# A spectral filter and a gated feed-forward block on one core: two sums per channel moved on VectorE, a cosine issued earlier, column transforms moved ahead of the gates

## Chip, cores and metric

The kernel runs on one core of one Trainium2 chip. The metric is device time in microseconds (us), the median of several runs. Engines are named as in the profile: PE is TensorE (matmuls; PEld its weight loads), DVE is VectorE, ACT is ScalarE, POOL is GpSimd, SP is SyncE, which here only issues DMAs.

## What is computed

The input is one matrix of 2048 rows by 576 columns in bf16. The reference, cut to what matters:

```
X = rfft2(layernorm(x)) * (w_r + 1j * w_i)       # over rows and columns
h = x + irfft2(X)
n = layernorm(h)
out = h + (gelu(n @ w_gate) * (n @ w_up)) @ w_down    # 576 -> 4608 -> 576
```

The Fourier transforms are done as matmuls with tables of sines and cosines. The 2048 rows are split as 16 x 128, so that a transform over rows is a 16-point step, a turn by a table, and a 128-point step.

## The kernel before, in words

All engines run hand-ordered queues: the order in the source is the order on each engine, and the tile framework only adds the waits. There are four PSUM tiles of two banks each under the tag "two" (helper `two`, line 66). Every stage below takes its PSUM from this ring. The tiles are handed out in the order in which the program releases them, so allocation number m waits for release number m - 4.

**Start (to about 25 us).** Layer norm of the rows, the 16-point step (`row16`), and the tables. The table TF holds, per channel, minus sine, cosine and sine; it is built in two parts, `first` (two channels) and `rest` (seven). For `rest` the steps are: `angle_a`, `angle_b`, `angle_c` on DVE, `sine` and `cosine` on ACT (lines 252 to 256), `minus_sine` on DVE, and then `turn_tf`, a DMA that writes the turned table TI (line 261).

**Spectral loop (lines 674 to 712, about 25 to 59 us).** The rows' spectrum is handled in eight channels in the order 1, 2, 3, 4, 5, 6, 7, 0; channel k goes together with k + 8. For one channel:

- `f2` (L479) on PE: the transform over columns, six matmuls; `f2_out` (L490) evicts it as `pq`, on ACT except for k = 9, which DVE evicts in two halves.
- `f3` (L496, L497) on PE: two halves of four matmuls with TF. ACT evicts them as `g` and `hs` (L518), except that channel 1's second half stays in PSUM and channel 0's halves are copied straight to `xab`.
- `sums_of` (L527, L528) on DVE: the difference and the sum of `g` and `hs`, which make `xab`.
- `wmul` on DVE: two products with the weights WR and WI (L547, into m1 and m2), `parts` (L552 za, L553 zb), and two writes of the block Zt: the first, L566, and the second, which is not issued there but kept in the list `held` and issued by `release` (L534) behind the two products of the next channel. In channels 6 and 7 it is released at once. Channel 0 is different: it is cut in two column pieces, each with two products and two writes (L575, L578).
- `i3` (L596; L620 for channel 0) on PE: the inverse step from Zt and TI; ACT evicts it into EO (L604, L609). Channels 1 to 4 make EO[0], channels 0 and 5 to 7 make EO[1].

In pass i of the loop PE's order is f2 of channel i, both f3 halves of channel i - 1, f2 of channel i's partner k + 8, then i3 of channel i - 3. DVE's order within `wmul(k, nxt)` before is: product 1, product 2, the previous channel's held write, za, zb, both sums of the next channel, the first Zt write.

**Column transforms.** `inv_cols(x, g)` (L647, ten matmuls on PE) is one inverse transform over columns, x = 0 or 1 for EO[x], g = 0 to 7. ACT evicts it (L660, L669), one of them DVE (L667). Before: (0,0), (0,1), (0,2), then i3 of channel 7, (0,3), (0,4), i3 of channel 0, (0,5), (1,0), (1,1), the 16-point step `add_rows(0)` (L773), (0,6), (0,7), (1,2) to (1,5); the last two, (1,6) and (1,7), stand in the head, described next.

**Feed-forward.** `gate` (L901 to L910): 18 matmuls of one tile of 128 hidden columns, gelu on ACT, product on DVE into P_sb. The rows go in four chunks of 512. Chunk 0 begins with a head of NH = 9 tiles that take only its first 256 rows (lines 912 to 923), so that gates can run before rows 256 to 511 are turned by DMA (`flip`). The main loop then gives these NH tiles their other 256 rows and every later tile all 512. Between the gates of chunk 0, the list `todo`, numbered by the main loop's tile (from 0), issues the remaining rows' work: `fold` (L759, L760, four instructions on DVE), `add_both` (eight matmuls L773 into two PSUM tiles, and two additions L784 on DVE), `stats2` (L116 to L118). Tile 1 has fold(2); tile 4 add_both(2); tile 5 and 6 one stats2 each; tile 6 also fold(3); tile 10 add_both(3) and fold(4). After 36 tiles the down matmuls (L946) follow, then the next chunk.

Of the kernel before, what the change touches and what calls it, by code (L numbers as in the profile page):

```python
# [9 lines left out]
ACT = mybir.ActivationFunctionType  # L10
ALU = mybir.AluOpType
FP32 = mybir.dt.float32
BF16 = mybir.dt.bfloat16
# [7 lines left out]
P = 128  # L21
# [4 lines left out]
J = D // 2 + 1  # L26
JP = J + 1
# [5 lines left out]
JW = 58  # L33
NW = JP // JW
# [3 lines left out]
Y_SCALE = 2.0 / (S * D) / G_SCALE  # L38
# [3 lines left out]
def kernel_body(  # L42
# [12 lines left out]
    V = nc.vector  # L55
    A = nc.scalar
# [9 lines left out]
    def two(name):  # L66
        return psum.tile([P, 2, 512], FP32, name=name, tag="two", bufs=4)
# [83 lines left out]
    WR = sp.tile([P, H + 1, JP], BF16, name="WR")  # L151
    WI = sp.tile([P, H + 1, JP], BF16, name="WI")
# [69 lines left out]
    def drop_sign(dst, src):  # L222
        V.tensor_scalar(
            dst.bitcast(I32),
            src.bitcast(I32),
            1,
            1,
            op0=ALU.logical_shift_left,
            op1=ALU.logical_shift_right,
        )  # L230
# [18 lines left out]
    def angle_c(sl):  # L249
        drop_sign(ab[:, sl], ab[:, sl])  # L250
# [4 lines left out]
    def cosine(sl):  # L255
        A.activation(TF[:, sl, 1, :], ab[:, sl], ACT.Sin, bias=nhpib[:], scale=2.0 * PI / S)
# [98 lines left out]
    first, rest = slice(0, 2), slice(2, 9)  # L355
# [88 lines left out]
    for sign in range(2):  # L444
# [4 lines left out]
            scale=G_SCALE if sign == 0 else -G_SCALE,  # L449
# [5 lines left out]
    wk = spw.__enter__()  # L455
    m1, m2 = (wk.tile([P, 2, 2, JP], BF16, name=n) for n in ("m1", "m2"))
# [5 lines left out]
    xab = {}  # L462
    gk, hk = {}, {}
    zt = {}
    order = [1, 2, 3, 4, 5, 6, 7, 0]
# [6 lines left out]
    def f2(c):  # L472
        ps = two("pq_ps")
        col = slice(slot[c] * P, (slot[c] + 1) * P)
        steps = [(par, t) for par in range(2) for t in (par, par + 2, 4)]
        if c == order[0]:
            steps.sort(key=lambda s: s[1] == 4)
        for par, t in steps:
            T.matmul(  # L479
                ps[:, par, 0:JP],  # L480
                lhsT=Bt[:, t, col],
                rhs=DT[:, t // 2, par] if t < 4 else DF[:, par],
                start=(t == par),
                stop=(t == 4),
            )
        pq[c] = wk.tile([P, 2, JP], BF16, name="pq", tag="pq", bufs=6)
        pq_ps[c] = ps
# [33 lines left out]
            return  # L521
        hk[k] = gh

    def sums_of(k):
        g, hs = gk[k], hk[k]
        x = xab[k] = wk.tile([P, 2, 2, JP], BF16, name="xab", tag="xab", bufs=2)
        V.tensor_tensor(x[:, 0, :, 0:J], g[:, :, 0:J], hs[:, :, 0:J], ALU.subtract)  # L527
        V.tensor_tensor(x[:, 1, ::-1, 0:J], g[:, :, 0:J], hs[:, :, 0:J], ALU.add)  # L528

    held = []  # L530

    def release():
        while held:
            V.tensor_tensor(*held.pop())  # L534

    def wmul(k, i, nxt=None):


        x = xab[k]
        z = Zts[i % 3]  # L540
        zt[k] = z
        zv = z[:].rearrange("p a w b j -> p a b w j")[:, :, :, :, 0:JW]
        sl = slice(k, 18 - k, 17 - 2 * k) if k else slice(0, 9, 8)

        def times(w, m, js):
            n = js.stop - js.start
            V.tensor_tensor(  # L547
                m[:, :, :, js], x[:, :, :, js], w[:, sl, js].unsqueeze(1).to_broadcast([P, 2, 2, n]), ALU.mult
            )

        def parts(za, zb, s):
            V.tensor_tensor(za, m1[:, 0, :, s], m2[:, 1, :, s], ALU.subtract)  # L552
            V.tensor_tensor(zb, m1[:, 1, :, s], m2[:, 0, :, s], ALU.add)  # L553

        def blocks(t):
            return t.rearrange("p b (w j) -> p b w j", j=JW)

        if k:
            times(WR, m1, slice(0, J))
            times(WI, m2, slice(0, J))  # L560
            release()
            za, zb = (wk.tile([P, 2, JP], BF16, name=n, tag=n, bufs=2) for n in ("za", "zb"))
            parts(za[:], zb[:], slice(0, JP))
            if nxt:
                sums_of(nxt)
            V.tensor_tensor(zv[:, :, 0], blocks(za[:]), blocks(zb[:, ::-1]), ALU.add)  # L566
            held.append((zv[:, :, 1], blocks(zb[:]), blocks(za[:, ::-1]), ALU.subtract))
            if k in order[5:7]:
                release()
            return  # L570
        for w0, w1 in ((0, 2), (2, NW)):
            lo, hi = w0 * JW, w1 * JW
            times(WR, m1, slice(lo, min(hi, J)))
            times(WI, m2, slice(lo, min(hi, J)))
            V.tensor_tensor(  # L575
                zv[:, 0, :, w0:w1], blocks(m1[:, 0, :, lo:hi]), blocks(m2[:, 1, :, lo:hi]), ALU.subtract
            )
            V.tensor_tensor(  # L578
                zv[:, 1, :, w0:w1], blocks(m1[:, 1, :, lo:hi]), blocks(m2[:, 0, :, lo:hi]), ALU.add
            )  # L580

    eo = {}

# [55 lines left out]
    cw = {}  # L639

    def inv_cols(x, g):

        ps = two("cs_ps")
        for w in range(NW):
            for e in range(2):
                rows = slice(64 * e, 64 * e + JW)
                T.matmul(  # L647
                    ps[:, e, 0:JP],
                    lhsT=EO[x][rows, w, 2 * g : 2 * g + 2].rearrange("p h e k l -> p (h e k l)"),
                    rhs=DQ[rows, w] if w or e else DT[rows, 0, :, 0, :],  # L650
                    start=(w == 0),
                    stop=(w == NW - 1),
                )
        pv = ps[:, :, 0:JP].rearrange("p t (q a) -> p t q a", q=2)
        if g >= 2:
            if x == 0 or g == 2:
                cw[x, g] = eop.tile([P, 2, JP], FP32, name=f"cw{x}{g}")[:]
            else:
                cw[x, g] = cwb[:, g - 3]
            A.activation(  # L660
                cw[x, g].rearrange("p t (a q) -> p t q a", q=2), pv, ACT.Copy, scale=Y_SCALE
            )
            return
        ts = eop.tile([P, 2, JP], BF16, name=f"cs{x}{g}")
        dst = ts[:].rearrange("p t (a q) -> p t q a", q=2)
        if x == 1 and g == 1:
            V.tensor_scalar(dst, pv, Y_SCALE, None, op0=ALU.mult)  # L667
        else:
            A.activation(dst, pv, ACT.Copy, scale=Y_SCALE)  # L669
        cs[x, g] = ts  # L670
# [4 lines left out]
    for i in range(n + 1):  # L675
        last = i >= n
        if not last:
            f2(order[i])
            if i != 1:
                f2_out(order[i])  # L680
        if i == 0:
            f2(order[0] + 8)
            for r in range(2):
                f2_out(order[0] + 8, V.tensor_copy, slice(r, r + 1))
            angle_c(rest)
            minus_sine(rest)

        if 1 <= i <= n:
            f3(order[i - 1], 0)
            f3(order[i - 1], 1)  # L690
            if i == 1:
                f2_out(order[1])
                sums_of(order[0])
            else:
                if i == 2:
                    cosine(rest)
                    turn_tf(rest)
                    pre = [load_gu(g) for g in range(3)]
                    nc.sync.dma_start(wd_a[:], wd_view[:, 0:NWA, :])
                wmul(order[i - 2], i - 1, order[i - 1])  # L700
        if not last and i:
            f2(order[i] + 8)
            f2_out(order[i] + 8)
        if i >= 3:
            for s in range(3):
                i3(order[i - 3], s)
        if last:
            wmul(order[i - 1], i)
        if i == 1:
            scr_pool.__exit__(None, None, None)  # L710
            eop = ctx.enter_context(tc.tile_pool(name="eop", bufs=1, side="right"))
            EO = [eop.tile([P, 5, H, 2, 4, 8], BF16, name=f"EO{x}", tag=f"EO{x}") for x in range(2)]
    for g in (0, 1, 2):
        inv_cols(0, g)
    for s in range(3):
        i3(order[6], s)
    for g in (3, 4):
        inv_cols(0, g)
    for s in range(3):
        i3(order[7], s)  # L720
    inv_cols(0, 5)

    spw.__exit__(None, None, None)
    spec.__exit__(None, None, None)
# [130 lines left out]
    y0 = add_rows(0)  # L855
    add_sum(0, y0)
    add_sum(1, y0, squares=False)
    for x, g in ((0, 6), (0, 7), (1, 2), (1, 3), (1, 4), (1, 5)):
        inv_cols(x, g)
    A.activation(keep.tile([P, 1], FP32, name="first_gelu")[:], zerob[:], ACT.Gelu_apprx_tanh)  # L860
    junk = roll.tile([P, D], BF16, name="junk", tag="junk", bufs=2)
# [47 lines left out]
        A.activation(g_sb, gu[:, 0, 0:n], ACT.Gelu_apprx_tanh)  # L909
        V.tensor_tensor(p_sb(f)[:, lo:hi], g_sb, gu[:, 1, 0:n], ALU.mult)  # L910

    NH = 9
    after = {
        0: [(sum_squares, 3), (norm2, 2), (flip, 2)],
        1: [(head_rstd, 3)],
# [1 line left out]
    }  # L917
    for f in range(NH):
        gate(0, f, groups[f // FQ], f % FQ, 0, 2 * P)
        for fn, h in after.get(f, ()):  # L920
            fn(h)
        if 2 <= f <= 3:
            inv_cols(1, f + 4)
    for tcnk in range(4):
        for gi in range(NG):
            for i in range(FQ):
                f = gi * FQ + i
                gate(tcnk, f, groups[0], i, 2 * P if tcnk == 0 and f < NH else 0, 4 * P)
                for fn, h in todo.pop(blk, ()):
# [95 lines left out]
```

## Time and profile before

| | us |
|---|---|
| median of 3 runs (lowest, highest) | 498.76 (498.66, 498.78) |
| the profiled execution's own time | 498.63 |
| its span, first to last instruction | 496.9 |
| PE busy in the span | 487.9 (98%) |
| DVE busy | 223.9 (45%) |
| ACT busy | 161.7 (33%) |
| granted TensorE clock, mean | 0.999 |
| gate matmuls L901 on the chain that ended last | 56% |
| down matmuls L946 on that chain | 27% |

Times in the timeline count from the span's start. A row gives the start, the duration, the engine, the line, the operation, the tiles written and read, and, in brackets, how long the engine stood idle before it and what ended that. Durations of two successive rows of one engine overlap: an engine takes up the next instruction a little before the last one's end, so what an instruction costs its engine is the distance between two starts. For example, a sum on DVE lasts 0.46 us, but the next one starts 0.37 us after it.

### The profile page before, as it was taken

How to read it: one execution, taken by the hardware profiler on the slowest of the kernel's cores; microseconds unless marked ns; L12 is line 12 of the kernel's file. 1: busy time of each engine (PE TensorE's matmuls, PEld its weight loads, DVE VectorE, ACT ScalarE, POOL GpSimd, SP SyncE). 2: the span in 40 equal slices, each digit the busy share in tenths (PEclk: the TensorE clock that was granted, in tenths of full speed). 3: DMA queues.
4: the chain of work that ended last, by engine and by line, in shares of the span. 5: the costliest groups of instructions: out<-in, count | busy, mean ns of one | idle time of the engine just before them, and what ended most of it. 6: DMA issues, size and time to landing. Idle time of an engine off the chain costs nothing.

```text
span 496.9 us, 12651 instructions
## 1 busy us (share of the span) xinstructions
PE 487.9 (98%) x5662; PEld 357.5 (72%) x5662; DVE 223.9 (45%) x443; ACT 161.7 (33%) x287; POOL 29.2 (6%) x78
## 2 busy tenths in 40 slices
PE   6999999999999999999999999999999999999997
PEld 3467789888879965555599955555899655555995
DVE  8999786888541245433311254333221333333111
ACT  8989973222311022232300122323110223233000
POOL 8500010211100000000000000000000000000000
PEclk9999999999999999999999999999999999999999
DMA  8729789859990019997730079987700277770000
GB/s 279 226 59 196 206 148 228 158 114 205 214 203 9 2 58 208 190 174 152 151 74 2 3 171 200 181 160 149 145 1 3 77 154 159 155 152 1 15 15 24
DMA packets 89549, 62.33 MB, mean 125 GB/s; under 512 B 23190, under 2 KB 88086, under 8 KB 89494
## 3 DMA queue, kind: packets, MB, share of 16 engines
q1 hardware_dynamic: 89206, 60.34, 60.8%
q0 software_dynamic: 288, 1.18, 0.7%
q8 instruction: 44, 0.72, 0.7%
q14 instruction: 11, 0.09, 0.1%
HBM read 52.65 MB, written 2.36 MB: 111 GB/s over the span
## 4 chain that ended last, share of the span: by engine, by line
PE 92%; ACT 0%; issue 0%; DVE 0%
PE gu L901 56%; PE acc L946 27%; PE cs_ps L647 2%; PE acc L965 2%; PE eo_ps L596 2%; PE pq_ps L479 1%; PE y_ps L773 1%; PE gh_ps L497 0%; PE gh_ps L496 0%; PE eo_ps L620 0%; PE pt L842 0%; ACT g L518 0%; ACT pq L490 0%; ACT hs L518 0%; DVE h_sb L972 0%
## 5 line engine op out<-in xcount | busy, mean ns | idle before, releaser
L901 PE MATMUL gu<-Bt,wgu 64*128 64x512 bf16 (+1 forms) x2646 | 271.9, 363 | 0.0
L901 PEld LDWEIGHTS <-wgu 64*128 64x128 bf16 x2646 | 162.1, 94 | 106.2 <-DMA wgu<-in_B_w_up_dram 0.3
L910 DVE TENSOR_TENSOR P_sb<-g_sb,gu 128x512 bf16<-128x512 f32 (+1 forms) x153 | 99.8, 654 | 143.3 <-ACT g_sb L909 143.3
L909 ACT ACTIVATE g_sb<-gu 128x512 f32<-128x512 f32 (+1 forms) x153 | 87.5, 572 | 193.6 <-PE gu L901 193.3
L946 PEld LDWEIGHTS <-P_sb 64*128 64x128 bf16 x2160 | 132.7, 94 | 0.5
L946 PE MATMUL acc<-wd,P_sb 64*128 64x288 bf16 x1440 | 93.5, 283 | 0.0
L955 DVE TENSOR_TENSOR part<-part,acc 128x576 f32<-128x576 f32 x15 | 11.3, 755 | 111.3 <-ACT part L954 111.3
L946 PE MATMUL acc<-wd_a,P_sb 64*128 64x288 bf16 x720 | 49.4, 283 | 0.0
L954 ACT COPY part<-acc 128x576 f32<-128x576 f32 x15 | 9.6, 639 | 122.4 <-PE acc L946 122.4
L798 DVE TENSOR_SCALAR hrow<-h_sb,mv,rstd 128x1152 bf16<-128x1152 bf16 x14 | 12.2, 868 | 0.6 <-POOL rstd L836 0.6
L479 PE MATMUL pq_ps<-DT,Bt 128*128 128x290 bf16 x64 | 12.3, 287 | 0.0
L901 PE MATMUL gu<-Bt,wgu_e 64*128 64x512 bf16 x108 | 12.2, 376 | 0.0
L286 PE MATMUL f2t<-h_sb,ident 128*128 128x512 bf16 x27 | 8.4, 471 | 3.7 <-DMA h_sb<-in_A_x_dram 3.7
L133 POOL TENSOR_TENSOR rstd<-rstd,mhalf 128x1 f32<-128x1 f32 (+1 forms) x16 | 11.6, 725 | 1.3
L957 DVE TENSOR_TENSOR h_sb<-h_sb,part 128x576 bf16<-128x576 bf16 x15 | 11.4, 758 | 0.5
L901 PEld LDWEIGHTS <-wgu_e 64*128 64x128 bf16 x108 | 10.0, 94 | 1.4
L479 PEld LDWEIGHTS <-Bt 128*128 128x128 bf16 x96 | 9.2, 97 | 2.5
L647 PE MATMUL cs_ps<-DQ,EO 58*128 58x290 bf16 x144 | 11.0, 283 | 0.0
L298 PE MATMUL f2t<-F,xn 128*128 128x256 bf16 x64 | 9.2, 275 | 0.8 <-DVE xn L136 0.8
L490 ACT CAST pq<-pq_ps 128x580 bf16<-128x580 f32 x15 | 9.8, 665 | 0.2
L132 POOL TENSOR_SCALAR rstd<-mv 128x1 f32<-128x1 f32 (+1 forms) x16 | 3.8, 240 | 99.8 <-DVE mv L118 99.5
L647 PEld LDWEIGHTS <-EO 58*128 58x128 bf16 x160 | 8.3, 94 | 1.9 <-issue 0.4
(139 smaller groups left out, 283.6 us busy)
## 6 DMA issues: line engine op xcount, KB each, us to landing
wgu<-in_B_w_gate_dram SPq DMA_DIRECT2D x46, 432.0 KB
wgu<-in_B_w_up_dram SPq DMA_DIRECT2D x46, 432.0 KB
wd_a<-in_B_w_down_dram SPq DMA_DIRECT2D x1, 1728.0 KB
wd<-in_B_w_down_dram SPq DMA_DIRECT2D x1, 1728.0 KB
wd<-in_B_w_down_dram SPq DMA_DIRECT2D x6, 288.0 KB
out_dram<-h_sb SPq DMA_DIRECT2D x3, 576.0 KB
h_sb<-in_A_x_dram SPq DMA_DIRECT2D x4, 288.0 KB
h_sb<-in_A_x_dram SPq DMA_DIRECT2D x2, 576.0 KB
```

Of the source, the lines that this page charges most:

```text
L133: G.tensor_tensor(dst[:, sl], dst[:, sl], mhalf[:, sl], ALU.pow)
L479: T.matmul(ps[:, par, 0:JP], lhsT=Bt[:, t, col], rhs=DT[:, t // 2, par] if t < 4 else DF[:, par], start=(t == par), stop=(t == 4),)
L596: T.matmul(pv[:, n], lhsT=z[:, a, w].rearrange("p b j -> p (b j)"), rhs=TI[:, ts[k], 1 - a : 3 - a, :], start=(a == 0), stop=(a == 1),)
L647: T.matmul(ps[:, e, 0:JP], lhsT=EO[x][rows, w, 2 * g : 2 * g + 2].rearrange("p h e k l -> p (h e k l)"), rhs=DQ[rows, w] if w or e else DT ...
L798: V.tensor_scalar(hrow[:], h_sb[:, h, :].rearrange("p (r k) -> p r k", k=64).unsqueeze(2).to_broadcast([P, NR, 2, 64]), mv2[:, h, 0:1], rs ...
L901: T.matmul(gu[:, c, 0:n], lhsT=w[rows, r, i * P : (i + 1) * P], rhs=hl[tcnk % 2][rows, r, lo:hi], start=(r == 0), stop=(r == NR - 1),)
L909: A.activation(g_sb, gu[:, 0, 0:n], ACT.Gelu_apprx_tanh)
L910: V.tensor_tensor(p_sb(f)[:, lo:hi], g_sb, gu[:, 1, 0:n], ALU.mult)
L946: T.matmul(accs[i][:, c, 0:DH], lhsT=p_sb(f)[rows, st * P : (st + 1) * P], rhs=wd[f // NWA][rows, f % NWA, c * DH : (c + 1) * DH], start=( ...
L955: V.tensor_tensor(part, part, accs[1][:, :, 0:DH], ALU.add)
L957: V.tensor_tensor(hv, hv, part, ALU.add)
L965: T.matmul(acc[:, 0, 0:DH], lhsT=p_sb(f)[:, st * P : (st + 1) * P], rhs=wd[f // NWA][:, f % NWA, cc], start=(f == 0), stop=(f == NFT - 1),)
```

## The change

Five edits, all in the order of the work; no computation is added or dropped.

1. `held` and `release` go. The second Zt write follows the first at once. The two sums of the next channel, before side by side between zb and the first Zt write, are dealt out: the difference behind the two products, the sum behind zb.
2. Channel 0 is no longer cut: two products over all columns, two writes.
3. `cosine(rest)` is issued in pass 0, behind `f2_out` of channel 1 on ACT, instead of in pass 2. `angle_c(rest)` moves ahead of DVE's two copies for k = 9, since the cosine reads its result.
4. (0,5) and (0,6) go ahead of i3 of channel 0, so that seven transforms stand before it; (0,7) follows it; (1,2) to (1,7) follow `add_rows(0)`. None is left in the head. DVE evicts (0,6) instead of ACT.
5. NH becomes 11.

```diff
     def wmul(k, i, nxt=None):
...
+        times(WR, m1, slice(0, J))
+        times(WI, m2, slice(0, J))
         if k:
-            times(WR, m1, slice(0, J))
-            times(WI, m2, slice(0, J))
-            release()
+            if nxt:
+                sum_of(nxt, 0)
             za, zb = (wk.tile([P, 2, JP], BF16, name=n, tag=n, bufs=2) for n in ("za", "zb"))
-            parts(za[:], zb[:], slice(0, JP))
+            parts(za[:], zb[:])
             if nxt:
-                sums_of(nxt)
+                sum_of(nxt, 1)
             V.tensor_tensor(zv[:, :, 0], blocks(za[:]), blocks(zb[:, ::-1]), ALU.add)
-            held.append((zv[:, :, 1], blocks(zb[:]), blocks(za[:, ::-1]), ALU.subtract))
-            if k in order[5:7]:
-                release()
-            return
-        for w0, w1 in ((0, 2), (2, NW)):
...
+            V.tensor_tensor(zv[:, :, 1], blocks(zb[:]), blocks(za[:, ::-1]), ALU.subtract)
+        else:
+            V.tensor_tensor(zv[:, 0], blocks(m1[:, 0]), blocks(m2[:, 1]), ALU.subtract)
+            V.tensor_tensor(zv[:, 1], blocks(m1[:, 1]), blocks(m2[:, 0]), ALU.add)
...
         if i == 0:
             f2(order[0] + 8)
+            angle_c(rest)
+            cosine(rest)
             for r in range(2):
                 f2_out(order[0] + 8, V.tensor_copy, slice(r, r + 1))
-            angle_c(rest)
             minus_sine(rest)
...
-                    cosine(rest)
                     turn_tf(rest)
...
-    for g in (3, 4):
+    for g in (3, 4, 5, 6):
         inv_cols(0, g)
     for s in range(3):
         i3(order[7], s)
-    inv_cols(0, 5)
+    inv_cols(0, 7)
...
-    for x, g in ((0, 6), (0, 7), (1, 2), (1, 3), (1, 4), (1, 5)):
+    for x, g in [(1, g) for g in range(2, 8)]:
         inv_cols(x, g)
...
-    NH = 9
+    NH = 11
...
-        if 2 <= f <= 3:
-            inv_cols(1, f + 4)
```

`sum_of(k, half)` is `sums_of` split in two: half 0 allocates `xab` and writes the difference, half 1 writes the sum.

More of the change, by code (lines that the diff above doesn't have):

```diff
@@ L522, in f3, with sum_of @@
         hk[k] = gh
-    def sums_of(k):
+    def sum_of(k, half):
         g, hs = gk[k], hk[k]
[L526 to L534, printed above, removed]
+        if half == 0:
+            xab[k] = wk.tile([P, 2, 2, JP], BF16, name="xab", tag="xab", bufs=2)
+        x = xab[k]
+        V.tensor_tensor(
+            x[:, 1, ::-1, 0:J] if half else x[:, 0, :, 0:J],
+            g[:, :, 0:J],
+            hs[:, :, 0:J],
+            ALU.add if half else ALU.subtract,
+        )
     def wmul(k, i, nxt=None):
@@ L549, in times, with parts @@
             )
-        def parts(za, zb, s):
-            V.tensor_tensor(za, m1[:, 0, :, s], m2[:, 1, :, s], ALU.subtract)
-            V.tensor_tensor(zb, m1[:, 1, :, s], m2[:, 0, :, s], ALU.add)
+        def parts(za, zb):
+            V.tensor_tensor(za, m1[:, 0], m2[:, 1], ALU.subtract)
+            V.tensor_tensor(zb, m1[:, 1], m2[:, 0], ALU.add)
         def blocks(t):
             return t.rearrange("p b (w j) -> p b w j", j=JW)
+        times(WR, m1, slice(0, J))
+        times(WI, m2, slice(0, J))
         if k:
-            times(WR, m1, slice(0, J))
-            times(WI, m2, slice(0, J))
-            release()
+            if nxt:
+                sum_of(nxt, 0)
             za, zb = (wk.tile([P, 2, JP], BF16, name=n, tag=n, bufs=2) for n in ("za", "zb"))
-            parts(za[:], zb[:], slice(0, JP))
+            parts(za[:], zb[:])
             if nxt:
-                sums_of(nxt)
+                sum_of(nxt, 1)
             V.tensor_tensor(zv[:, :, 0], blocks(za[:]), blocks(zb[:, ::-1]), ALU.add)
-            held.append((zv[:, :, 1], blocks(zb[:]), blocks(za[:, ::-1]), ALU.subtract))
-            if k in order[5:7]:
-                release()
-            return
-        for w0, w1 in ((0, 2), (2, NW)):
[L572 to L580, printed above, removed]
+            V.tensor_tensor(zv[:, :, 1], blocks(zb[:]), blocks(za[:, ::-1]), ALU.subtract)
+        else:
+            V.tensor_tensor(zv[:, 0], blocks(m1[:, 0]), blocks(m2[:, 1]), ALU.subtract)
+            V.tensor_tensor(zv[:, 1], blocks(m1[:, 1]), blocks(m2[:, 0]), ALU.add)
     eo = {}
@@ L659, in inv_cols @@
                 cw[x, g] = cwb[:, g - 3]
-            A.activation(
-                cw[x, g].rearrange("p t (a q) -> p t q a", q=2), pv, ACT.Copy, scale=Y_SCALE
-            )
+            dst = cw[x, g].rearrange("p t (a q) -> p t q a", q=2)
+            if x == 0 and g == 6:
+                V.tensor_scalar(dst, pv, Y_SCALE, None, op0=ALU.mult)
+            else:
+                A.activation(dst, pv, ACT.Copy, scale=Y_SCALE)
             return
@@ L692, in kernel_body @@
                 f2_out(order[1])
-                sums_of(order[0])
+                sum_of(order[0], 0)
+                sum_of(order[0], 1)
             else:
                 if i == 2:
-                    cosine(rest)
                     turn_tf(rest)
```

## The prediction, made blind

> **What bounds the kernel now.** I read the page's first part, then the windows by stage, then the timelines of DVE, ACT and PE around each edit.
>
> ```profile
> PE 487.9 (98%) x5662; PEld 357.5 (72%) x5662; DVE 223.9 (45%) x443; ACT 161.7 (33%) x287; POOL 29.2 (6%) x78
> ```
>
> Over the whole span PE is the bound, and behind the spectral loop its queue runs on almost without idle time. So an edit counts only through PE's idle time. The loop itself reads differently. Columns of the windows: length, then busy us of PE, PEld, DVE, ACT, POOL, then clock, DMA share, GB/s.
>
> ```profile
> 32.00:36.00 4.00, 3.00 (x23) 1.85 (x21) 4.00 (x10) 3.66 (x6) 0.00 (x0) 1.00 0.28 57
> 40.00:44.00 4.00, 4.00 (x37) 3.25 (x34) 4.00 (x10) 3.88 (x8) 0.00 (x0) 1.00 1.12 214
> 48.00:52.00 4.00, 4.00 (x35) 3.08 (x33) 4.00 (x11) 3.91 (x8) 0.00 (x0) 1.00 1.13 203
> ```
>
> From 40 to 52 us PE **and** DVE are full. By starts, one channel costs DVE two products of 0.67 and six adds of 0.37, 3.57 us; PE 20 matmuls (f2, f3) of 0.124 and ten (i3) of 0.109, also 3.57. At 32 to 36 PE idles 1 us, and DVE doesn't. PE's idle time, by its timeline:
>
> ```profile
> 32.80 0.30 PE L496 MATMUL gh_ps<-pq,TF 128*128 128x289 bf16 x1 [0.27 <-ACT TF L256]
> 33.33 0.28 PE L497 MATMUL gh_ps<-pq,TF 128*128 128x289 bf16 x1 [0.23 <-ACT pq L490]
> 35.61 0.60 PE L596 MATMUL eo_ps<-TI,Zt 128*128 128x256 bf16 x4 [0.51 <-ACT hs L518]
> ```
>
> By distance of starts less 0.12, these lost 0.43 (the cosine), 0.41 (a `pq` that stood behind the cosine on ACT) and 0.67. The third row names ACT's `hs`, but that was done at 35.13; what ended just before 35.61 is DVE's held write:
>
> ```profile
> 34.38 0.76 DVE L547 TENSOR_TENSOR m<-xab,WI 128x1156 bf16<-128x1156 bf16 x1
> 35.05 0.46 DVE L534 TENSOR_TENSOR Zt<-zb,za 128x580 bf16<-128x580 bf16 x1
> ```
>
> It ends at 35.51. So edits 1 and 3 aim at 1.5 us of PE's idle time. The end of the loop decides whether that is kept. DVE, then PEld:
>
> ```profile
> 51.59 0.45 DVE L534 TENSOR_TENSOR Zt<-zb,za 128x580 bf16<-128x580 bf16 x1
> 52.10 0.99 PEld L596 LDWEIGHTS <-Zt 128*128 128x128 bf16 x10 [0.25 <-DVE Zt L534]
> ```
>
> Channel 6's i3 starts 0.06 behind the write that DVE ends at 52.04, and DVE has run without a gap since 28.78. **PE leaves the loop when DVE does.**
>
> **Edit 3, the cosine.** ACT:
>
> ```profile
> 26.72 0.64 ACT L490 CAST pq<-pq_ps 128x580 bf16<-128x580 f32 x1
> 28.10 0.64 ACT L518 CAST g<-gh_ps 128x578 bf16<-128x578 f32 x1 [0.74 <-PE gh_ps L497]
> 31.68 1.07 ACT L256 ACTIVATE TF<-ab,nhpib 128x896 bf16<-128x896 f32 x1
> ```
>
> `angle_c` (0.62) fits DVE's 0.56 of idle time ahead of 26.83: its input ends at 26.27, it runs from 26.30, its start-to-start 0.53 ends at 26.83. The cosine then starts at 26.72 + 0.54 = 27.26, and `g` 0.945 later (as 31.68 to 32.63), at 28.20 instead of 28.10. That `g` opens DVE's chain: first difference at 28.88 instead of 28.78. Cost: 0.10 at DVE's head. Gain on PE: channel 3's f3 no longer waits (32.38 instead of 32.80; a rest of 0.03 for `pq` stays). SP's order is unchanged: `turn_tf` stands behind thirteen small DMAs that SP issues until 33.98.
>
> **Edit 1, the sums.** Channel 1's products then start at 30.40 and 31.08. The next difference is wanted at 31.75, but its `hs` (ACT, 31.15 for 0.66) ends at 31.81: start 31.85, a new wait of 0.09. It replaces a gap of 0.19 before (product 2 from 30.98 to za at 31.84 instead of 0.67 later, since za reads product 2 directly). Then za 32.22, zb 32.59, sum 32.96, writes 33.33 and 33.70, next product 34.07. Before, the products started at 33.70 with a write of 0.37 still owed, which is 34.07 too. From there the instruction count is the same, 3.57 us per channel: channel 7's first product comes at 34.07 + 5 x 3.57 = 51.93, against 51.96. **DVE gains 0.03.**
>
> Behind the waiting difference on DVE are za and zb. In later channels `hs` is early enough: PE runs ahead, channel 3's `hs` ends near 34.3 for a difference at 35.42, and from channel 4 on the margin is 0.7 us.
>
> PE: i3 of channel 1 now waits for a write that ends at 34.16: start 34.24, 1.37 earlier. It keeps this lead at 3.57 us per channel until its two f3 halves of channel 0 end at 50.62. Then i3 of channel 6 wants the write that ends at 51.56 + 0.46 = 52.02: start 52.07. **The lead of 1.37 turns into a wait of 1.45 there**; net gain 0.03.
>
> By occupancy this reads otherwise. The Trainium skill, Perfetto Trace Analysis, section "Identifying the Most-Contended Engine", tells to improve the engine with the highest occupancy and to look for gaps on it; by the page that is PE, and its gaps of 1.5 us would be the gain: 497.1 without the other edits. The windows above do not bear that out for this stage, where DVE has none to give; the same page's "Optimization Strategy" allows for regimes with different engines.
>
> **Edits 2 and 4.** Uncut, channel 0 costs DVE 0.67 + 0.79 + 0.37 + 0.46 from 55.08: done at 57.4, against 57.95. PE asks for it later than before (57.83): i3 of channel 7 at 55.25, four transforms of 0.62, so 59.0. Nothing waits for DVE there, before or after; the 0.21 between the matmuls at each of the four changes between i3 and transforms (53.09 to 53.30 is one) is the same whoever is named, so I read 0.08 of it as a switch that stays. With two transforms in place of four, PE would be at 57.8 and still not wait. The two transforms leave the head, where each took 0.63 (71.03 to 71.66): gain 0.02. Evictions keep up: the one given to DVE (about 0.82, as L667) ends at 60.0, for a PSUM tile wanted at 60.3. The loads of `wgu_e` wait for i3 of channel 0 and issue 1.2 later, near 60.5; their traffic, which ended near 70.5 in the windows, ends near 72. The head's tiles 9 and 10 now read them, from 78.
>
> **Edit 5, NH.** A half tile takes PE 0.983 (180 matmuls in 9.83), a whole one 1.943 (108 in 11.65): two tiles cut cost 2 x (1.966 - 1.943) = 0.05. But the cut also speeds PE through tiles 9 and 10 while DVE is behind:
>
> ```profile
> 88.73 0.45 DVE L759 TENSOR_TENSOR both<-cwb 128x288 bf16<-128x288 f32 x1
> 89.10 0.45 DVE L760 TENSOR_TENSOR both<-cwb 128x288 bf16<-128x288 f32 x1
> 89.47 0.75 DVE L910 TENSOR_TENSOR P_sb<-g_sb,gu 128x256 bf16<-128x256 f32 x2
> 90.39 0.69 DVE L910 TENSOR_TENSOR P_sb<-g_sb,gu 128x512 bf16<-128x512 f32 x1 [0.17 <-ACT g_sb L909]
> ```
>
> DVE is full from 83.81 to 90.2 with add_both(2), two stats2 and fold(3); only then come the products of tiles 7 and 8 (ends 89.88 and 90.21). PE:
>
> ```profile
> 83.58 4.19 PE L901 MATMUL gu<-Bt,wgu 64*128 64x256 bf16 x72
> 87.51 4.15 PE L901 MATMUL gu<-Bt,wgu_e 64*128 64x512 bf16 x36
> 91.40 0.75 PE L773 MATMUL y_ps<-both,G 64*128 64x288 bf16 x8
> ```
>
> Tiles 9 and 10 take 3.89 whole, 1.97 as halves. So, counted from the main loop's start, add_both(3) comes at 91.40 - 1.92 = 89.48, with its second matmul at 89.58. By the ring its two PSUM tiles are those of tiles 7 and 8. Tile 8's is free at 90.21, plus 0.06 to 0.10 as at the waits above: **a new wait of 0.70 us**. Afterwards DVE is ahead and PE waits no more: tile 11's PSUM (tile 9's, 90.54) is free when PE gets there at 90.7.
>
> The bounds of this term: 0, if the tiles handed out are others; 1.4, if tile 10's own product had to pass too (two half products of 0.33 behind 89.80, so 90.46 + 0.41 = 90.87; less 89.58, plus 0.1). I take 0.70, since the rows of tiles 7 and 8 give it.
>
> **Sum**, on the profiled execution (498.63, of which 496.9 span and 1.7 around it): - 0.03 (DVE's chain) - 0.02 (head) + 0.05 (halves) + 0.70 (wait) = + 0.70: 499.33. The median of the runs shown is 0.13 above that execution: **499.4 to 499.5; I say 499.4**, + 0.14%. A difference of about 0.2%, 1.0 us, is what I take as measurable.
>
> **Rivals.**
> - *The wait at tile 10 doesn't come* (a PSUM tile is free earlier): 498.76 + 0.0 = 498.8. Against it stand the two DVE rows; for it, that no row of before shows that wait.
> - *The lead is kept* (the rule above as a mechanism: the loop is PE's, DVE shortens with the dealt order): - 1.4 for the three waits. With the wait at tile 10, 498.0; without, 497.4. Against it: DVE's gapless chain.
> - *Slower: the early difference waits in every channel.* It stands 1.34 us into the channel's DVE time, before 2.45; `hs` came only 0.03 to 0.13 ahead of it in rows 39.76 to 50.48. If PE does not get its lead of 1.37 (say the cosine lands later, or `hs` stays where it was), DVE loses 1.11 less 0.1 once, then runs in step. It decides when channel 3's `hs` ends later than 35.4; I expect 34.3. Price + 1.0, all on PE behind channel 6: 500.4.
> - *The change does not do what it says*: the waits at 32.80, 33.33 and 35.61 remain; without lead or loss the time is that of my forecast within 0.1, since DVE sets the end.
>
> **Chances.** Forecast (499.0 to 499.8) 0.62; no wait at tile 10: 0.13; lead kept: 0.05 with and 0.05 without that wait; difference late: 0.12; the rest, 0.03, slower for a cause not seen. The range takes in the forecast, the case without the wait and the late difference, 0.87: 498.6 to 500.5. Faster by over 0.2% (under 497.8) is the lead kept without the wait, 0.05, and a little of that with it, 0.02: 0.07. Slower (over 499.8): 0.12 + 0.03 and the forecast's upper edge 0.03: 0.18. Within: 0.75.
>
> **What would show it.** Right: `g` of channel 1 near 28.2; i3 of channel 1 near 34.2; PE idle for about 1.4 ahead of i3 of channel 6, which starts within 0.1 of 52.1; no idle time at i3 of channel 0; PE idle 0.6 to 0.8 within add_both(3), released by DVE's P_sb. Wrong: DVE idle ahead of differences from channel 3 on; i3 of channel 6 ahead of 51.5; add_both(3) without a wait.

## The result, and the profile after

The changed kernel takes **499.53 us** (median of 22 runs, 499.15 to 500.5); 22 runs of the kernel before beside them gave 498.67 (498.44 to 499.34). The ratio is 1.0018, with a 95% interval of 1.0012 to 1.0025: slower by 0.86 us, where + 0.7 was forecast. The profiled execution took 499.36, 0.17 below the median; its span is 497.6 (before 496.9).

The whole start lies about 0.1 us earlier in this execution (the first f3 matmul starts at 27.32, before at 27.41), so times forecast on the old time axis are read here less 0.1. The windows of the loop in the kernel after, columns as before (length, busy us of PE, PEld, DVE, ACT, POOL, clock, DMA share, GB/s):

```profile
32.00:36.00 4.00, 4.00 (x35) 3.04 (x34) 4.00 (x10) 3.50 (x6) 0.00 (x0) 1.00 0.63 59
...
48.00:52.00 4.00, 2.74 (x25) 2.01 (x23) 4.00 (x10) 3.82 (x7) 0.00 (x0) 1.00 1.13 200
```

PE's idle microsecond at 32 to 36 is gone, and 1.26 us of idle time have come up at 48 to 52, where PE was full. DVE is full in both windows, before and after.

**Where PE gained.** PE's timeline at the first i3:

```profile
32.28 0.28 PE L496 MATMUL gh_ps<-pq,TF 128*128 128x289 bf16 x1
32.43 0.28 PE L497 MATMUL gh_ps<-pq,TF 128*128 128x289 bf16 x1
...
33.91 0.28 PE L479 MATMUL pq_ps<-DF,Bt 128*128 128x290 bf16 x1
34.16 1.25 PE L587 MATMUL eo_ps<-TI,Zt 128*128 128x256 bf16 x10
```

The first two starts are 0.15 apart (0.12 is normal: the 0.03 foretold), and i3 of channel 1 starts at 34.16 instead of 35.61, 0.13 late against its predecessor. The waits of 0.43, 0.41 and 0.67 are gone. DVE at the same place:

```profile
28.77 1.43 DVE L529 TENSOR_TENSOR xab<-g,gh_ps 128x578 bf16<-128x578 bf16 x2 [0.85 <-ACT g L518]
...
30.97 0.76 DVE L547 TENSOR_TENSOR m<-xab,WI 128x1156 bf16<-128x1156 bf16 x1
31.75 0.47 DVE L529 TENSOR_TENSOR xab<-g,hs 128x578 bf16<-128x578 bf16 x1
...
33.61 0.45 DVE L568 TENSOR_TENSOR Zt<-zb,za 128x580 bf16<-128x580 bf16 x1
```

The early difference starts 0.78 behind the second product instead of 0.67: it waits for `hs` by 0.11, once. The second write now stands behind the first and ends at 34.06; i3 starts 0.10 behind it.

**Where PE lost it.** First DVE, then PE, at the end of the loop:

```profile
51.46 0.46 DVE L568 TENSOR_TENSOR Zt<-zb,za 128x580 bf16<-128x580 bf16 x1
```

```profile
50.43 0.29 PE L497 MATMUL gh_ps<-pq,TF 128*128 128x289 bf16 x1
51.98 1.27 PE L587 MATMUL eo_ps<-TI,Zt 128*128 128x256 bf16 x10 [1.26 <-DVE Zt L568]
```

From 50.43 to 51.98 are 1.55 us, of which a matmul costs 0.12: PE waits 1.43 for the write that ends at 51.92. Counted from the first f3, i3 of channel 6 starts at 24.66, before at 24.69. All of PE's lead is gone but 0.03.

**Where the time went.** DVE, then PE, around add_both(3) in the feed-forward:

```profile
90.93 0.45 DVE L754 TENSOR_TENSOR both<-cwb 128x288 bf16<-128x288 f32 x1
91.30 1.41 DVE L904 TENSOR_TENSOR P_sb<-g_sb,gu 128x256 bf16<-128x256 f32 x4
```

```profile
89.35 2.23 PE L895 MATMUL gu<-Bt,wgu_e 64*128 64x256 bf16 x36
91.77 0.98 PE L767 MATMUL y_ps<-both,G 64*128 64x288 bf16 x8 [0.19 <-DVE P_sb L904]
```

The four products on DVE are those of tiles 7 to 10; they stand in DVE's queue behind all of fold(3). Tile 7's ends at 91.72 and lets add_both(3) start at 91.77; tile 8's ends at 92.05 and lets its second matmul start at 92.10. These two matmuls start 0.463 and 0.330 behind their predecessors. In add_both(2) of the same kernel, which waits for nothing, the same two steps are 0.006 and 0.103. So 0.46 and 0.23 are lost, **0.68 us** in all. The bracket names only 0.19, since modelled matmul ends hide the rest; the distance of starts shows it.

A second, small loss was not foretold. The list of waits of the kernel after has

```profile
PEld L895 <- DMA wgu<-in_B_w_up_dram: 0.4, 1, 0.4
```

The gate matmul at 137.00 starts 0.315 behind the one at 136.69, and its tile of 18 matmuls takes 0.11 longer than the 1.94 of the others: lost to a weight load (before, this wait of PEld was 0.3 and cost PE nothing).

From anchor to anchor (us):

| from, to | before | after | difference |
|---|---|---|---|
| first f3 to i3 of channel 6 | 24.69 | 24.66 | - 0.03 |
| to the first gate | 15.99 | 17.23 | + 1.24 (two more transforms) |
| to the first down matmul | 74.32 | 73.91 | - 0.41 |

The two transforms take 1.25 out of the third stretch; 0.68 for the wait, 0.11 for the load and 0.05 for the cut tiles come in, which makes the - 0.41. The sum of the three stretches is + 0.80.

### The profile page after: what moved, and what is told of

Its sections match the earlier page's. It is cut to its first block, busy times and chain, and to the rows that moved or that the text cites. A ratio compares the mean times of both kernels' runs of the same rounds, so it can differ in the third digit from the quotient of the medians.

```text
span 497.6 us, 12727 instructions
## 1 busy us (share of the span) xinstructions
PE 487.6 (98%) x5698; PEld 340.2 (68%) x5698; DVE 224.5 (45%) x442; ACT 161.6 (32%) x288; POOL 28.9 (6%) x78
## 4 chain that ended last, share of the span: by engine, by line
PE 88%; DVE 7%; DMA 2%; SPq 1%; ACT 1%; issue 0%
PE gu L895 55%; PE acc L938 27%; PE cs_ps L638 2%; PE acc L957 2%; DVE m L547 2%; DMA h_sb<-in_A_x_dram 1%; PE y_ps L767 1%; SPq L421 1%; DVE xab L529 1%; DVE xn L136 1%; DVE st L117 1%; DVE st L116 1%; DVE Zt L567 0%; PE eo_ps L587 0%; ACT Bt L322 0%
## 5 line engine op out<-in xcount | busy, mean ns | idle before, releaser
L895 PEld LDWEIGHTS <-wgu 64*128 64x128 bf16 x2646 | 144.8, 94 | 123.6 <-DMA wgu<-in_B_w_up_dram 0.4
L895 PE MATMUL gu<-Bt,wgu_e 64*128 64x256 bf16 (+1 forms) x144 | 12.5, 322 | 0.0
L587 PE MATMUL eo_ps<-TI,Zt 128*128 128x256 bf16 x70 | 8.8, 273 | 1.3 <-DVE Zt L568 1.3
L123 ACT ACTIVATE junk<-h_sb 128x576 bf16<-128x576 bf16 x14 | 9.4, 678 | 0.4 <-DMA h_sb<-in_A_x_dram 0.4
```

The lines of the kernel that those rows point to most:

```text
L895: T.matmul(gu[:, c, 0:n], lhsT=w[rows, r, i * P : (i + 1) * P], rhs=hl[tcnk % 2][rows, r, lo:hi], start=(r == 0), stop=(r == NR - 1),)
```

## The experiments

**Theory.** (W) What makes the change slower is the wait in add_both(3), which comes from NH = 11 together with the folds ahead of it in DVE's queue. (D) Edits 1 and 3 give PE a real lead of 1.4 us, and it is worth nothing as DVE ends the loop and PE has nothing else to do there. **Rivals**: the loss lies in the cut tiles or the moved loads and not in that wait; PE's idle 1.43 us is harmless and what PE does there doesn't matter; the lead isn't the edits' doing.

Runs of the kernel before stand beside every experiment's (medians 498.54 to 498.62); ratios are to these.

**1. NH = 11 alone, on the kernel before**

```diff
-    NH = 9
+    NH = 11
```

> The kernel before with NH = 11 alone, no other edit. Theory W: the waits of 0.4 and 0.2 us appear in add_both(3) here too, so 0.6 to 0.7 us over before: 499.3 to 499.4. Rival L: no change, 498.7.

Measured: 499.35 (499.19 to 499.6), ratio 1.0014 [1.0005, 1.0023]. PE's timeline:

```profile
91.80 0.98 PE L773 MATMUL y_ps<-both,G 64*128 64x288 bf16 x8 [0.19 <-DVE P_sb L910]
```

Steps of 0.463 and 0.332 at the two first matmuls, as in the changed kernel (0.463 and 0.330). From the first f3 to the first down matmul: 115.71, before 115.00, after 115.80. One constant gives nearly all of the loss, with none of the other four edits.

**2. The folds ahead of the wait, on the changed kernel.** fold(2) and fold(3) go from the main loop's tiles 1 and 6 into the head, behind its tiles 6 and 8.

```diff
-            todo.setdefault((1, 6, 10, 13, 16, 19)[h // 2 - 2], []).append((fold, h // 2))
+            if h > 6:
+                todo.setdefault((10, 13, 16, 19)[h // 2 - 4], []).append((fold, h // 2))
...
+        6: [(fold, 2)],
+        8: [(fold, 3)],
```

> The changed kernel with fold(2) and fold(3) issued in the head, behind tiles 6 and 8, where DVE idles 0.56 us per tile, in place of tiles 1 and 6 of the main loop. Theory W: DVE is no longer behind at tile 7, the waits in add_both(3) go, nothing else moves: 0.6 us off the changed kernel, 498.9. Rival L: no change, 499.5.

Measured: 498.71 (498.46 to 499.61), ratio 1.0004 [0.9995, 1.0013]. PE's timeline (this execution began 0.87 us later than that of the changed kernel):

```profile
90.22 2.23 PE L896 MATMUL gu<-Bt,wgu_e 64*128 64x256 bf16 x36
92.19 0.75 PE L767 MATMUL y_ps<-both,G 64*128 64x288 bf16 x8
```

add_both(3) starts 1.97 us behind the first of the 36 half matmuls of tiles 9 and 10, and two half tiles take 2 x 0.983; in the changed kernel it was 2.42. No bracket is left. First f3 to first down matmul: 115.17, 0.63 less than after: the wait's 0.68 is gone, and the late weight load costs 0.16 here instead of 0.11. The medians differ by 0.82, the lowest runs by 0.69. The wait goes with its cause, so (W) holds against the cut tiles, which are still there.

**3. Fewer tiles cut: NH = 10, and NH = 9**

```diff
-    NH = 11
+    NH = 10
```

> The changed kernel with NH = 10 in place of 11, nothing else. Theory W (the loss is PE's wait in add_both(3), since tiles 9 and 10 as halves bring PE there before DVE has released the PSUM of tiles 7 and 8): tile 10 is whole again, PE arrives 0.96 us later, the waits of 0.40 and 0.23 in add_both(3) are gone; but the second halves now begin at about 79.0 us, where the turned rows land at about 79.2, so up to 0.4 of it may come back there: 498.9 to 499.3. Rival L (the loss is in the spectral loop, the wait of 1.4 us ahead of channel 6's i3): no change, 499.5.

Measured: 499.27 (498.85 to 499.84), ratio 1.0011 [1.0002, 1.0020]. The wait in add_both(3) is gone, but PE's timeline has another:

```profile
79.94 5.09 PE L895 MATMUL gu<-Bt,wgu 64*128 64x256 bf16 x90 [0.53 <-DMA Bt<-hrow]
```

The matmul at 79.94 starts 0.80 behind the one at 79.14, and its tile loses 0.80 us: the head ends before the rows turned by DMA are there. The last DMA packets of the turn end at 79.2, but in the trace its last semaphore update comes at 79.81, and PE goes on 0.13 behind that. The expectation went by the packets and allowed 0.4. From the first f3 to the first down matmul this kernel takes 115.78, the changed one 115.80: what one wait gives back the other takes.

```diff
-    NH = 11
+    NH = 9
```

> The changed kernel with NH = 9. Theory W: no wait in add_both(3), but with no transforms left in the head the second halves begin at 78.05 us, ahead of the turned rows (79.2): a new wait of 1.1 to 1.3 us on a DMA in its place, 500.0 to 500.2. Rival L: no change, 499.5. A third view, that NH is of no matter: 499.5 too.

Measured: 500.08 (499.81 to 500.42), ratio 1.0028 [1.0017, 1.0039]. The step from the matmul at 78.31 to the next, at 80.00, loses 1.69, where 1.1 to 1.3 were expected:

```profile
80.00 4.21 PE L895 MATMUL gu<-Bt,wgu 64*128 64x256 bf16 x74 [1.42 <-DMA Bt<-hrow]
```

Here too PE goes on 0.13 behind the turn's last semaphore update (79.87). In the changed kernel that update comes at 79.78, in the kernel before at 77.93.

So edit 5 isn't a slip. With two transforms taken out of the head, it needs two more tiles until the rows are there; with 11 tiles the main loop starts at 80.01 without a wait, 0.10 behind the time at which it could. The cover has a price of 0.68 further on, and without it edit 4 costs 0.80 (10) or 1.69 (9) at once.

**4. The wait at the loop's end filled.** The transforms (0,0) and (0,1) go ahead of i3 of channel 6; three then stand ahead of channel 7's, two ahead of channel 0's. Alone on the changed kernel:

```diff
+        if last:
+            for g in (0, 1):
+                inv_cols(0, g)
...
-    for g in (0, 1, 2):
+    for g in (2, 3, 4):
...
-    for g in (3, 4, 5, 6):
+    for g in (5, 6):
```

> The changed kernel with the filled wait alone, the folds where the change has them. Theories D and W together: 1.25 us off the changed kernel's 499.5 and the waits of 0.6 in add_both(3) stay: 498.2 to 498.3, so that the two repairs add up. If PE's wait in add_both(3) grew or vanished because PE comes earlier: 497.5 or over 498.8.

Measured: 498.10 (497.91 to 498.96), ratio 0.9988 [0.9979, 0.9997]; add_both(3)'s steps of 0.46 and 0.33 stay. Together with the folds of experiment 2:

> The changed kernel with the folds in the head (as before) and PE's order at the loop's end changed: transforms (0,0) and (0,1), whose input has been ready since channel 4, go ahead of channel 6's i3, into PE's wait; (0,2) to (0,4) then stand before channel 7's i3, (0,5) and (0,6) before channel 0's. Theory D: PE's lead of 1.4 us is real, it was only lost for want of other work; 1.24 us of transforms fill the wait, channel 0's i3 starts near 57.7 instead of 58.95, and the time is 497.4 to 497.5, faster than both kernels. Rival P: the order doesn't matter, 498.7 as with the folds alone.

Measured: **497.44** (497.22 to 498.27), ratio 0.9976 [0.9966, 0.9986]: faster than both kernels. PE's timeline at the loop's end:

```profile
50.64 0.29 PE L497 MATMUL gh_ps<-pq,TF 128*128 128x289 bf16 x1
50.87 0.79 PE L638 MATMUL cs_ps<-DQ,EO 58*128 58x290 bf16 x9
51.50 0.78 PE L638 MATMUL cs_ps<-DQ,EO 58*128 58x290 bf16 x9
52.22 1.26 PE L587 MATMUL eo_ps<-TI,Zt 128*128 128x256 bf16 x10
```

The whole start lies 0.2 later in this execution (first f3 27.53). The transforms run where PE had waited, and i3 of channel 6 is not held up by them: it starts 24.69 behind the first f3. By medians the folds give 0.8, the fill 1.4, both 2.1. So (D) holds: PE's idle time there was real, and other work put into it uses it.

The same fill on the kernel before:

```diff
+        if last:
+            for g in (0, 1):
+                inv_cols(0, g)
...
-    for g in (0, 1, 2):
+    for g in (2,):
```

> The kernel before with the same two transforms ahead of channel 6's i3, no other edit. Theory D: PE had no lead there (its wait was 0.11 us), so at most 0.1 us comes off: 498.5 to 498.6. A third view, that the order of the transforms is worth something by itself: as much as in the changed kernel, 1.2 us off, 497.4.

Measured: 498.65 (498.52 to 499.05), ratio 1.0002 [0.9993, 1.0011]. i3 of channel 6 moves to 53.44, 1.34 later, about what the two transforms take: with no lead there is nothing to fill.

**5. Which edit makes the lead.** Each kernel is that of folds and fill with one edit undone.

Edit 1 undone:

```diff
         times(WI, m2, slice(0, J))
         if k:
-            if nxt:
-                sum_of(nxt, 0)
+            release()
...
+                sum_of(nxt, 0)
                 sum_of(nxt, 1)
...
-            V.tensor_tensor(zv[:, :, 1], blocks(zb[:]), blocks(za[:, ::-1]), ALU.subtract)
+            held.append((zv[:, :, 1], blocks(zb[:]), blocks(za[:, ::-1]), ALU.subtract))
+            if k in order[5:7]:
+                release()
```

> The same kernel (497.44), with edit 1 undone: sums side by side, the second write held behind the next channel's products. Theory D: channel 1's i3 waits for the held write at 35.6 again and PE has no lead left, whatever the cosine does, so the filling transforms only push channel 6's i3 back: all of the 1.25 us is lost, 498.7. Rival: the early cosine alone made the lead, 497.4 to 498.0.

Measured: 498.81 (498.66 to 499.5), ratio 1.0005 [0.9996, 1.0014]. i3 of channel 1 is back at 35.58, and i3 of channel 6 comes late:

```profile
53.41 1.27 PE L595 MATMUL eo_ps<-TI,Zt 128*128 128x256 bf16 x10
```

Edit 3 undone:

```diff
-            angle_c(rest)
-            cosine(rest)
             for r in range(2):
                 f2_out(order[0] + 8, V.tensor_copy, slice(r, r + 1))
+            angle_c(rest)
...
+                    cosine(rest)
                     turn_tf(rest)
```

> The kernel with folds in the head and filled wait (497.44), with edit 3 undone: angle_c and the cosine are back in their places of before. Theory D: PE loses 0.43 and 0.41 us at channel 3's f3 again, its lead at channel 1's i3 is 0.7 instead of 1.4 us, so the filling transforms end near 52.6 instead of 51.9 and channel 6's i3 is late by 0.6: 498.0. Rival: the dealt order alone made the lead, 497.4.

Measured: 498.09 (497.96 to 498.33), ratio 0.9986 [0.9977, 0.9995]. PE's waits of 0.43 (for the cosine) and 0.41 (for the `pq` behind it) are back, i3 of channel 1 starts at 34.84, that of channel 6 at 52.62.

Edit 2 undone (channel 0 in two pieces again):

```diff
+            for w0, w1 in ((0, 2), (2, NW)):
...
+                times(WR, m1, slice(lo, min(hi, J)))
+                times(WI, m2, slice(lo, min(hi, J)))
```

> The same kernel (497.44), with edit 2 undone: channel 0 cut in two column pieces again. DVE ends it near 58.0 instead of 57.4, and PE asks for its first piece at 57.7, for the second at 58.2. Theory D: no wait, 497.4 within 0.1. Rival (the uncut channel was needed): a wait of 0.3 to 0.6 at channel 0's i3, 497.7 to 498.0.

Measured: 497.47 (497.28 to 497.72), ratio 0.9975 [0.9964, 0.9985]; i3 of channel 0 at 57.94 waits for nothing.

So without edit 1 the fill gives nothing (498.81); edit 3 is worth 0.65 of the lead beside it; edit 2 nothing.

**6. Is DVE the bound of the loop?** Four of its sums are left out of DVE's queue, so that part of the spectrum is missing, and memsets on POOL stand in.

```diff
+        if half and k in (3, 4, 5, 6):
+            G.memset(x[:, 1, :, 0:J], 0.0)
+            return
```

> The changed kernel without the sums of channels 3 to 6: each is left out, and POOL writes zeros in its place, so that part of the spectrum is lost; DVE has four adds of 0.37 us less inside the loop. Theory D (DVE sets the end of the loop, and edits 1 and 3 only moved PE's idle time to the wait ahead of channel 6's i3): that wait of 1.4 us goes, channel 6's i3 starts near 50.6, and 1.4 us come off: 498.1 by the median of the changed kernel (499.5). Rival P (PE or ACT sets the loop's pace, DVE's adds are covered): no change, 499.5.

Measured: 498.54 (498.39 to 499.43), ratio 1.0000 [0.9991, 1.0009]: faster than the changed kernel by 1.0, less than expected. Counted from the first f3, i3 of channel 6 comes 0.72 earlier and not 1.48 (4 x 0.37). DVE's timeline shows why:

```profile
36.29 0.45 DVE L556 TENSOR_TENSOR zb<-m,m 128x580 bf16<-128x580 bf16 x1
36.78 0.46 DVE L570 TENSOR_TENSOR Zt<-za,zb 128x580 bf16<-128x580 bf16 x1
```

With the sum between them gone, the write that reads zb starts 0.49 behind it, not 0.37 (up to 0.56 in other channels): the sum had covered 0.12 to 0.19 of waiting for a result, 0.61 in the four channels. Channel 7's difference waited 0.12 for its `hs` besides. Together these are 0.73 of the 0.76 that are missing. The direction is that of DVE as the bound: what came off DVE's chain came off PE's wait, whose bracket is 0.59 instead of 1.26. The size of the expectation was wrong. From the first f3 to the first down matmul the gain is 0.84, since the late weight load costs nothing here.

**7. Work of DVE handed to POOL**

```diff
-        V.tensor_tensor(
+        (G if k in (3, 4, 5, 6) and not half else V).tensor_tensor(
```

> The changed kernel with the differences of channels 3 to 6 on POOL, which is idle in the loop; nothing is left out. Theory D: if POOL works beside DVE, four adds of 0.37 us come off DVE's chain and up to 1.4 us off the whole: 498.1. If the two engines hinder each other while both read SBUF (the Trainium skill, SBUF - State Buffer, section Who interferes with whom, says that a DVE instruction with two SBUF inputs contends with a POOL instruction that reads SBUF), DVE's adds and products grow longer by about what POOL takes, and nothing is gained or some is lost: 499.5 to 501. Rival P: 499.5.

Measured: 502.6 (502.46 to 502.74), ratio 1.0078 [1.0065, 1.0092]. POOL, then DVE:

```profile
38.50 1.87 POOL L529 TENSOR_TENSOR xab<-g,hs 128x578 bf16<-128x578 bf16 x1 [1.74 <-ACT hs L518]
```

```profile
38.48 0.75 DVE L547 TENSOR_TENSOR m<-xab,WR 128x1156 bf16<-128x1156 bf16 x1
39.16 1.84 DVE L547 TENSOR_TENSOR m<-xab,WI 128x1156 bf16<-128x1156 bf16 x1
```

The product that starts 0.02 ahead of POOL's instruction keeps its 0.75; the one that starts while POOL computes takes 1.84 instead of 0.76 and ends at 41.00, 0.63 behind POOL's end at 40.37, about as if it had begun then. A za beside another of POOL's took 1.42 instead of 0.46. It goes the other way too: POOL's first of the four, at 34.52, took 2.24, where its shortest took 1.28, while two products of DVE kept their 0.76. i3 of channel 6 comes at 55.43. The Trainium skill, SBUF — State Buffer, section "Who interferes with whom", has the rule: a DVE instruction with two inputs from SBUF contends with a POOL instruction that reads SBUF, and not with one that only writes it. Both runs agree: beside the memsets of experiment 6 (0.58 us each on POOL) the adds kept 0.45 to 0.46.

## Why the prediction was right

- **DVE ends the loop: right, as the main step.** i3 of channel 6 was to keep 0.03 of 1.37; it kept 0.03 of the 1.35 by which i3 of channel 1 came earlier against the first f3. The wait was forecast at 1.45 and is 1.43. (The chain "without a gap" of before holds by the profile's brackets; by starts DVE waited 0.18 and 0.19 for its own results at 30.30 and 31.84, and the second of these is the gap that the prediction itself counts under edit 1.) Experiments 4 and 5 show that the lead existed and what it was worth.
- **Edit 3**: `g` of channel 1 was to come at 28.20 and the first difference at 28.88, so 28.10 and 28.78 on the new axis. ACT, kernel after:

```profile
27.14 1.06 ACT L256 ACTIVATE TF<-ab,nhpib 128x896 bf16<-128x896 f32 x1
28.09 0.65 ACT L518 CAST g<-gh_ps 128x578 bf16<-128x578 f32 x1
```

  So 28.09, and 28.77 for the difference (above). The cosine went into the 0.74 us for which ACT had waited ahead of `g`, and cost only what stood over.
- **Edit 1**: difference of channel 2 late by 0.11 (forecast 0.09), channel 7's first product at 51.83 (51.93 less 0.1), no wait at a difference in channels 3 to 6. The rival of the difference late in every channel did not come.
- **Edits 2 and 4**: i3 of channel 0 at 58.95 without a wait (59.0 forecast), DVE's eviction of (0,6) from 59.05 to 59.8 (to 60.0 forecast).
- **Edit 5**: the step was the wait of two PSUM tiles' releases in add_both(3), and its size is near the forecast: 0.68 for 0.70. The tiles are those of 7 and 8, as derived from the ring. Experiments 1 and 2 put it in and took it out.
- **What the sum lacked**: the weight load that costs 0.11 at 137.00. The prediction followed the moved `wgu_e` loads only up to the head. Whether it is these loads that make the later one late isn't shown: kernels that issue the same loads lose nothing there (experiment 4, both) or 0.16 (experiment 2).
- **Luck at the turned rows**: the prediction has no term for the rows that DMA turns. In the changed kernel they come 1.85 later than before (79.78 against 77.93), and the head ends 0.10 behind the time at which PE could take them. So the term is nothing, but by a margin that the prediction never looked at; experiment 3 shows what a shorter head would have cost.
- **From + 0.70 to + 0.86**: the three stretches give + 0.80, which is the forecast with 0.11 for the load and 0.02 less for the wait. The two profiled executions differ by only 0.73, mainly because that of the changed kernel reached its first f3 0.10 earlier; the medians differ by 0.13 more. These two partly cancel: that the time fits to 0.16 is in part luck, that the terms fit is not.
- **By occupancy** (the Trainium skill, Perfetto Trace Analysis, "Identifying the Most-Contended Engine"), PE's gaps would have been the gain, 497.1. They went and nothing came of it. The search for gaps itself stands in the same page's "Optimization Strategy", and there it goes by the regime of interest; in this one the windows show DVE as full as PE. The same section says that interleaving stages with different engines may improve performance. Experiment 4 did that, and it paid 1.4.

What stays open is what makes the weight load late in some of these kernels, and the 0.2 to 0.3 us by which some differences of medians (experiments 2, 3 and 6) exceed what the timelines account for. By the lowest runs the gains of experiments 2 and 6 are 0.69 and 0.76, near the timelines' 0.63 and 0.84, so the rest may lie in how late an execution starts: the profiled one of experiment 2 began 0.87 later than that of the changed kernel. No trace of the other runs shows it.

## What to carry to other kernels

Where two engines are full in one stage, follow a gap that you close to the end of that stage: the engine that ends it keeps what the other gained, unless other work is put where the first now waits. When tiles of a shared PSUM ring are made smaller, PE runs through them sooner, and the release that it needs may stand in another engine's queue behind work that had nothing to do with it; move that work ahead, or the tile's size back. A step taken out of a stage that covers a DMA has to be replaced by as much other work, and each of the two has its price; the time to cover runs to where the waiting engine is let go, here 0.7 us behind the last packet.

## What was unexpected of the hardware

An add on DVE (128x580, bf16) that reads the result of the one just before starts 0.49 to 0.56 us behind it (experiment 6), an independent one 0.37: taking work out of such a chain gives less than its step. An instruction of DVE beside a POOL `tensor_tensor` grew from 0.76 to 1.84 us and from 0.46 to 1.42, and POOL's own took 1.28 to 2.24. The 1.43 us of PE's idle time left its granted clock at 1.00 in that window.
